# A decode block on one core: one 128-column strip of w3 and one of wo, loaded by sixteen transfers of 15 down to 1 partitions and of 8

## The chip, the cores and the metric

The kernel runs on one core of a Trainium2 chip. The time is device microseconds of one launch. Before the change the median of three runs is 1302.96 us (1302.66 to 1303.77). All arrays are float32.

## The reference, cut to what matters

One token for each of 4 sequences goes through attention over a cache of 4096 positions and 32 heads, and beside it through a small MLP; both are added to the input.

```python
def _A_ref(x, k_cache, v_cache, wq, wo):
    B, Sq, D = x.shape                       # 4, 1, 512
    H, Dh = 32, 128                          # caches: B, H, 4096, Dh
    q = (x @ wq).reshape(B, Sq, H, Dh).transpose(0, 2, 1, 3)
    scores = jnp.einsum("bhqd,bhkd->bhqk", q, k_cache) * (Dh ** -0.5)
    p = _softmax(scores, axis=-1)
    o = jnp.einsum("bhqk,bhkd->bhqd", p, v_cache)
    return o.transpose(0, 2, 1, 3).reshape(B, Sq, H * Dh) @ wo

def _B_ref(x, w1, w2, w3, w4):               # with one token the shifted half adds zeros
    ...
    h2 = _gelu(_layernorm(x1, axis=-1) @ w3) @ w4       # w3: 512 x 1792, w4: 1792 x 512
    return x1 + h2

xn = _layernorm(x, axis=-1)
return x + _A_ref(xn, A_k_cache, A_v_cache, A_wq, A_wo) + _B_ref(xn, B_w1, B_w2, B_w3, B_w4)
```

With one token (S = 1) every shift of the token mixing moves in zeros, so `x1` is the MLP's input and w1 and w2 aren't read.

## The kernel before

**Tiles.** The 128 pairs of sequence and head are worked on four at a time, in 32 steps (`NJ`). A step's keys are one tile of 128 partitions by 64 KB (8.4 MB), loaded as one contiguous row for each partition, and so are its values. There are three such buffers of 64 KB for a partition: `ks[0]` and `ks[1]` for keys in turn, and `vs` for values. Everything else that is large borrows them. At the start w3 (28 KB for a partition) lies in `vs`, with x and the small arrays of the layernorms behind it, wq (64 KB) in `ks[1]`, and the first key tile in `ks[0]`. At the end the last value tile lies in the free key buffer, w4 in `vs`, and wo (64 KB) in `ks[LAST % 2]`, in place of the last keys.

**Engines in a step.** DVE multiplies the key tile by the query, spread over the partitions, in place, and sums over the 128 elements of a head, in two halves (L327 and L328). After each half it raises `summed`. Then it takes the maximum. ACT makes the exponentials (L346). PE multiplies them with the value tile (L380) and sums over partitions (L385, L387); ACT copies the two results out (L351, L353) and raises `done`. Loops on DVE, ACT and PE run by themselves over the 32 steps, tied by semaphores.

**Loads.** All large loads are issued by SP, in the order in which its program has them. At the start stand w3, wq and the first key tile, without a wait. They stand ahead of `tc.close()` and `tc.compile()`, lines 178 and 179, where all engines meet at a barrier; x is loaded by ACT's queue (L180) after that. Then SP has the second key tile (once the q matmuls are through with wq, `pq_ok`), the first value tile (once w3's part and the queries are done), and the third key tile in two halves, each as the half of its buffer has been summed. From there on SP alternates: key tile j + 2 once step j is summed, value tile j + 1 once step j is done. At the end come the last value tile, w4 once step 30 is done, and wo once step 31 is summed.

**Ahead of the steps.** From x two layernorms in a row are made, on DVE with a square root on ACT; `xn` is the attention's input, `x1n` the MLP's. PE transposes each (L213), multiplies `x1n` by w3 (L236), once `w3_in` is there, and then `xn` by wq (L257), once `wq_in` is there. Between them ACT and DVE make the GELU. The queries are scaled (L261), transposed and copied into `qT`; DVE's loop begins with a copy from it (L318).

**The end.** wo is loaded in seven transfers of falling size, each with a semaphore of its own: column blocks 0 to 16, 16 to 24, 24 to 28, 28 to 30, 30 (`wo_cuts`, L286), and the two halves of block 31 (L290). PE waits for each in turn and multiplies (L417, and L151 in `blocks4`, then L432), so that little is left to do when the last one lands. Two stores of half the result each end the program (L439).

**Helpers.** `do` (class `Steps`) records an operation on an engine with its waits. `load(o, i, sem, by, *after, queue="SP")` issues a transfer that adds 16 to `sems[sem]`, and returns the pair to wait for: that semaphore and the value `by`.

Of the kernel before, what the change touches and what calls it, by code (L numbers as in the profile page):

```python
# [44 lines left out]
P = 128  # L45
# [4 lines left out]
PE, DVE, ACT = mybir.EngineType.PE, mybir.EngineType.DVE, mybir.EngineType.Activation  # L50
# [38 lines left out]
def decode_block(ctx: ExitStack, tc: tile.TileContext, x, k, v, wq, wo, w3, w4, out):  # L89
    nc = tc.nc  # L90
    B, H, S, DH = k.shape
    D = wq.shape[0]
    F = w3.shape[1]
    NC = D // P
# [7 lines left out]
    WC = H * DH // P  # L102
    LAST = NJ - 1

    def sb(name, *shape):
        return nc.alloc_sbuf_tensor(name, [P, *shape], F32).ap()
# [4 lines left out]
    ks = [sb(f"ks{n}", R * DH) for n in range(2)]  # L111
    vs = sb("vs", R * DH)
# [35 lines left out]
    def blocks4(start, stop, w, m, src):  # L148

        for t in range(4):  # L150
            i = nc.tensor.matmul(total[32 * t:32 * t + m, :], w, src[:, P * t:P * t + P], start=start, stop=stop)  # L151
        return i

    do = Steps(nc)
    wo_sems = [nc.alloc_semaphore(f"wo{n}") for n in range(7)]
# [4 lines left out]
    wo_cuts = ((0, 16), (16, 24), (24, 28), (28, 30), (30, WC - 1))  # L160
# [3 lines left out]
    def load(o, i, sem, by, *after, queue="SP"):  # L164
        return do(queue, lambda e: e.dma_start(o, i), *after, done=(sems[sem], 16, by))

    do.owned = tc.no_tile_sem_insts
    w3_sb = vs[:, :NC * F].rearrange("p (c f) -> p c f", c=NC)
# [1 line left out]
    xs, lnc = spare[:B, :D], spare[:B, D:2 * D]  # L170
    ident, wide = spare[:, 2 * D:2 * D + P], spare[:, 3 * D:3 * D + NC * 8 * 32]
    wq_sb = ks[1].rearrange("p (c n) -> p c n", c=NC)
    w3_in = load(w3_sb, w3.rearrange("(p c) f -> p c f", c=NC), "w3", 16)
    wq_in = load(wq_sb, wq.rearrange("(p c) n -> p c n", c=NC), "wq", 16)
    k_in = {0: load(ks[0], rows(kf, 0), "k0", 16)}

# [105 lines left out]
    w4_in = load(w4_sb, w4.rearrange("(p m) n -> p m n", m=NF), "w4", 16, DONE[LAST - 1])  # L282
    do.wait("SP", [SUMMED[LAST]])
    wo_r = wo.rearrange("(p c) n -> p c n", c=WC)
    for (c0, c1), sem in zip(wo_cuts, wo_sems):
        nc.sync.dma_start(wo_sb[:, c0:c1], wo_r[:, c0:c1]).then_inc(sem, 16)  # L286
    half = D // 2
    for n, sem in enumerate(wo_sems[-2:]):
# [18 lines left out]
    with nc.Fori(0, NJ // 2, engines=OrderedEngineSet([DVE]), head_slot={DVE: 128}) as j:  # L307
        e, n = nc.vector, 0
# [92 lines left out]
    for m in range(NF):  # L401
        t, g, n = (m, g4[:, m, :], 32) if m < 4 else (m % 4, gT[:, m, :], B)
# [7 lines left out]
    ys = os.rearrange("p m d -> p (m d)")  # L410
    do.wait("PE", [X_ok])
    for (c0, c1), sem in zip(wo_cuts, wo_sems):
        do.wait("PE", [(sem, 16)])
        for c in range(c0, c1):
            if c < 24:
                t = (c + 2) % 4
                i = nc.tensor.matmul(y[32 * t:32 * t + B, :], X[:, c, :], wo_sb[:, c], start=False, stop=(c >= 20))  # L417
            else:
                i = blocks4(False, False, X[:, c, :], B, wo_sb[:, c])
        d = do("PE", lambda e: i)  # L420

        if c1 == 24:
            ys_ok = do("ACT", lambda e: e.copy(ys, y), d)
        elif c1 == 28:
            do.wait("PE", [ys_ok])
            blocks4(False, False, sel, 32, ys)
# [49 lines left out]
```

## Time and profile before

| | us |
|---|---|
| median of three runs | 1302.96 |
| lowest and highest run | 1302.66, 1303.77 |
| the profiled execution, whole | 1302.75 |
| its span, from the first to the last instruction | 1301.4 |

| engine | busy us | share of the span |
|---|---|---|
| DVE | 1164.6 | 89% |
| PE | 365.8 | 28% |
| ACT | 93.5 | 7% |
| POOL | 2.4 | 0% |

The profile is of one execution. PE, PEld (weight loads), DVE, ACT, POOL and SP are the engines; a name with q behind it (SPq) is an engine's sequencer, where DMA issues, waits and branches are. L236 is line 236 of the kernel. A row of the timeline has the start, the duration, the engine and line, what is written and read, the number of instructions merged into the row, and in brackets how long the engine had been idle and what released it. A row of stretches has the length, the busy time and number of instructions of PE, PEld, DVE, ACT and POOL, the granted share of TensorE's clock, the mean busy share of the core's 16 DMA engines, and GB/s. Packets of one DMA engine follow each other; a transfer lands when its semaphore is full.

The DMA moves 561.0 MB from HBM in one launch: 537 MB of keys and values, 8.4 MB each of wq and wo, and 3.7 MB each of w3 and w4.

### The profile page before, as it was taken

The numbers are of one execution on the slowest core, as the hardware profiler recorded it, in microseconds if no ns is written. First come the engines' busy times: TensorE is split into PE (matmuls) and PEld (weight loads), VectorE is DVE, ScalarE is ACT, GpSimd is POOL, SyncE is SP. The second block draws the span as 40 slices with busy tenths as digits, with TensorE's granted clock in tenths as the row PEclk, the third lists the DMA queues.
The fourth block names the chain that finished last, engine by engine and source line by source line (L and its number), as shares of the span: only waits on it lengthen the run. The fifth ranks groups of instructions, "written<-read, shape, count | busy, mean of one in ns | idle before, by whom it ended". The sixth has DMA issues, their size and how long they took to land. (4 is left out here: it accounts for less than half of the span.)

```text
span 1301.4 us, 6682 instructions
## 1 busy us (share of the span) xinstructions
PE 365.8 (28%) x2652; PEld 131.5 (10%) x2652; DVE 1164.6 (89%) x325; ACT 93.5 (7%) x332; POOL 2.4 (0%) x12
## 2 busy tenths in 40 slices
PE   3221233321233321232331133232123322122337
PEld 1000111100011110011110011110001110001112
DVE  3499999999999999999999999999999999999990
ACT  1000000000000000000000000000000000000001
POOL 0000000000000000000000000000000000000000
PEclk9656666655666665666665666665666665566668
DMA  9999999999999999999999999999999999999998
GB/s 403 445 423 447 425 441 425 435 435 431 437 427 443 427 441 425 437 431 435 435 425 443 427 443 425 441 427 433 435 433 437 425 443 427 441 425 437 431 429 369
DMA packets 10831, 561.10 MB, mean 431 GB/s; under 512 B 1212, under 2 KB 1476, under 8 KB 1736
## 3 DMA queue, kind: packets, MB, share of 16 engines
q1 hardware_dynamic: 10808, 561.00, 99.7%
q8 instruction: 4, 0.07, 0.0%
q14 instruction: 3, 0.02, 0.0%
q10 hardware_dynamic: 16, 0.01, 0.0%
HBM read 561.00 MB, written 0.01 MB: 431 GB/s over the span
## 5 line engine op out<-in xcount | busy, mean ns | idle before, releaser
L327 DVE TENSOR_TENSOR ks<-ks,qb 128x8192 f32<-128x8192 f32 x64 | 556.3, 8692 | 59.4 <-DVEq L295 54.4
L328 DVE TENSOR_REDUCE sc<-ks 128x64 f32<-128x8192 f32 x64 | 555.9, 8686 | 2.2
L380 PE MATMUL pv<-vs,pw 128*32 128x512 f32 x1984 | 280.4, 729 | 875.2 <-PEq L295 875.2
L380 PEld LDWEIGHTS pv<-vs,pw 128*32 128x32 f32 x1984 | 77.4, 131 | 1053.6 <-issue 1053.6
L351 ACT COPY os<-pv 128x512 f32<-128x512 f32 x32 | 18.7, 585 | 822.0 <-ACTq L295 822.0
L346 ACT ACTIVATE pw<-sc,small 32x128 f32<-32x128 f32 x128 | 51.0, 398 | 281.2 <-ACTq L295 280.0
L385 PE MATMUL poz<-sel,os 128*128 128x4 f32 x256 | 32.8, 252 | 28.1 <-PEq L295 28.1
L385 PEld LDWEIGHTS poz<-sel,os 128*128 128x128 f32 x256 | 31.0, 191 | 56.3 <-issue 56.3
L346 ACT ACTIVATION_READ_ACCUMULATOR pw<-sc,small 32x1 f32 x128 | 23.5, 184 | 0.0
L434 DVE COPY os<-total 4x128 f32<-4x128 f32 x2 | 0.6, 282 | 15.1 <-PE total L432 15.1
L333 DVE TENSOR_REDUCE small<-sc 128x1 f32<-128x128 f32 x32 | 9.2, 286 | 4.7
L361 DVE RECIPROCAL rz<-oz 128x96 f32<-128x96 f32 (+1 forms) x2 | 1.1, 553 | 13.4 <-ACT oz L353 13.3
L387 PE MATMUL poz<-rs,ones 128*128 128x4 f32 x64 | 11.7, 253 | 0.0
L319 DVE STREAM_TRANSPOSE qb<-qg 128x128 f32<-128x128 f32 x32 | 10.0, 311 | 1.1
L262 DVE STREAM_TRANSPOSE vs<-pw 128x1024 f32<-128x1024 f32 x1 | 1.2, 1246 | 10.4 <-ACT pw L261 10.4
L318 DVE COPY qg<-qT 128x4 f32 x32 | 5.5, 171 | 5.5 <-issue 4.7
L387 PEld LDWEIGHTS poz<-rs,ones 128*128 128x128 f32 x64 | 9.7, 192 | 0.0
L380 PE MATMUL pv<-ks,pw 128*32 128x512 f32 x64 | 9.3, 746 | 0.0
L353 ACT COPY oz<-poz 128x8 f32 x32 | 5.3, 165 | 50.9 <-ACTq L295 50.9
L213 PE MATMUL pt<-vs,pw 4*128 4x4 f32 x16 | 4.0, 372 | 15.8 <-DVE pw L207 15.8
L334 DVE STREAM_TRANSPOSE tr<-small 128x32 f32<-128x32 f32 x32 | 6.8, 212 | 1.1
L417 PE MATMUL y<-ks,X 128*4 128x512 f32 x48 | 7.0, 748 | 2.5 <-DMA ks<-in_A_wo_dram 2.5
(75 smaller groups left out, 72.5 us busy)
## 6 DMA issues: line engine op xcount, KB each, us to landing
ks<-in_A_k_cache_dram SPq DMA_DIRECT2D x2, 4096.0 KB, 26.9
vs<-in_B_w_dram SPq DMA_DIRECT2D x2, 3584.0 KB, 13.8
ks<-in_A_wo_dram SPq DMA_DIRECT2D x1, 4096.0 KB, 21.7
ks<-in_A_wo_dram SPq DMA_DIRECT2D x1, 2048.0 KB, 26.3
ks<-in_A_wo_dram SPq DMA_DIRECT2D x1, 1024.0 KB, 28.3
ks<-in_A_wo_dram SPq DMA_DIRECT2D x1, 512.0 KB, 29.1
ks<-in_A_k_cache_dram SPq DMA_DIRECT2D x31, 42.2
vs<-in_A_v_cache_dram SPq DMA_DIRECT2D x31, 27.0
```

Of the source, the lines that this page charges most:

```text
L318: step(e.tensor_copy(qg, pairs[:, s, bass.ds(j, 1)].rearrange("p o n -> p (o n)")))
L319: step(e.transpose(qb.rearrange("p (n m) -> p n m", m=HP), qg.unsqueeze(2).to_broadcast([P, DH // HP, HP])))
L327: step(e.tensor_tensor(out=kt, in0=kt, in1=qb.unsqueeze(1).to_broadcast([P, w, DH]), op=ALU.mult))
L328: step(e.reduce_sum(sc[s][:, c:c + w], kt, axis=AX.X))
L333: step(e.reduce_max(rm, sc[s], axis=AX.X))
L334: step(e.transpose(tr[s], rm.to_broadcast([P, HP])))
L346: i = nc.scalar.activation(pw[hp, :, 4 * h:4 * h + 4], sc[s][hp, :].rearrange("p (g w) -> p g w", w=4), AF.Exp, bias=small[hp, s, 1:2], sc ...
L351: nc.scalar.copy(os, pv.rearrange("p (m d) -> p m d", m=4)).then_inc(sems["copied"], 1)
L380: i = nc.tensor.matmul(pv[32 * t:32 * t + 32, :], pw[:, g, :], vt[:, 4 * g:4 * g + 4, :], start=(g < 4), stop=(g >= NG - 4))
L385: nc.tensor.matmul(poz[:, 0:G], os[:, m, :], sel.rearrange("p (h m) -> p m h", m=4)[:, m, 0:G], start=(m == 0), stop=(m == 3))
L387: nc.tensor.matmul(poz[:, G:2 * G], ones.to_broadcast([P, P]), rs, start=True, stop=True).then_inc(sems["poz"], 1)
L417: i = nc.tensor.matmul(y[32 * t:32 * t + B, :], X[:, c, :], wo_sb[:, c], start=False, stop=(c >= 20))
```

## The change

`strips` lists sixteen ranges of partitions, of 15, 14, and so on down to 1, and then 8: together 128.

w3 was one transfer of 128 rows of 28,672 bytes. It becomes one of 128 rows of 28,160 bytes, and sixteen transfers for the last 512 bytes of each row (128 columns of float32), one for each range of partitions. All add to the semaphore `w3`, and PE waits for 16 x 17 = 272 instead of 16. All seventeen are issued by SP ahead of wq.

wo's first transfer (column blocks 0 to 16) was 128 rows of 32,768 bytes. It becomes one of 32,256 bytes for each row, and sixteen transfers for the last 512 bytes of each row, with the same ranges. They are issued in its place, ahead of the other six transfers, and PE waits for 272 on that semaphore. Where the bytes come from and where they go in SBUF stays the same.

```diff
--- before.py
+++ after.py
@@ -170,7 +170,14 @@
     xs, lnc = spare[:B, :D], spare[:B, D:2 * D]
     ident, wide = spare[:, 2 * D:2 * D + P], spare[:, 3 * D:3 * D + NC * 8 * 32]
     wq_sb = ks[1].rearrange("p (c n) -> p c n", c=NC)
-    w3_in = load(w3_sb, w3.rearrange("(p c) f -> p c f", c=NC), "w3", 16)
+    sizes, strips = (*range(15, 0, -1), 8), []
+    for n in sizes:
+        p0 = strips[-1][1] if strips else 0
+        strips.append((p0, p0 + n))
+    w3_rows, n3 = w3.rearrange("(p c) f -> p (c f)", c=NC), NC * F - P
+    load(vs[:, :n3], w3_rows[:, :n3], "w3", 16)
+    for n, (p0, p1) in enumerate(strips):
+        w3_in = load(vs[p0:p1, n3:n3 + P], w3_rows[p0:p1, n3:], "w3", 16 * (n + 2))
     wq_in = load(wq_sb, wq.rearrange("(p c) n -> p c n", c=NC), "wq", 16)
     k_in = {0: load(ks[0], rows(kf, 0), "k0", 16)}
 
@@ -282,7 +289,11 @@
     w4_in = load(w4_sb, w4.rearrange("(p m) n -> p m n", m=NF), "w4", 16, DONE[LAST - 1])
     do.wait("SP", [SUMMED[LAST]])
     wo_r = wo.rearrange("(p c) n -> p c n", c=WC)
-    for (c0, c1), sem in zip(wo_cuts, wo_sems):
+    wo_rows, n0 = wo.rearrange("(p c) n -> p (c n)", c=WC), wo_cuts[0][1] * D - P
+    nc.sync.dma_start(ks[LAST % 2][:, :n0], wo_rows[:, :n0]).then_inc(wo_sems[0], 16)
+    for p0, p1 in strips:
+        nc.sync.dma_start(ks[LAST % 2][p0:p1, n0:n0 + P], wo_rows[p0:p1, n0:n0 + P]).then_inc(wo_sems[0], 16)
+    for (c0, c1), sem in zip(wo_cuts[1:], wo_sems[1:]):
         nc.sync.dma_start(wo_sb[:, c0:c1], wo_r[:, c0:c1]).then_inc(sem, 16)
     half = D // 2
     for n, sem in enumerate(wo_sems[-2:]):
@@ -410,7 +421,7 @@
     ys = os.rearrange("p m d -> p (m d)")
     do.wait("PE", [X_ok])
     for (c0, c1), sem in zip(wo_cuts, wo_sems):
-        do.wait("PE", [(sem, 16)])
+        do.wait("PE", [(sem, 16 * (1 + len(strips)) if c0 == 0 else 16)])
         for c in range(c0, c1):
             if c < 24:
                 t = (c + 2) % 4
```

## The prediction

> **What bounds the kernel now.** I read the page first: its DMA lines and the chain of waits.
>
> ```profile
> span 1301.4 us, 6682 instructions
> DMA  9999999999999999999999999999999999999998
> q1 hardware_dynamic: 10808, 561.00, 99.7%
> DVE 3%; DMA 2%; PE 0%; SPq 0%; issue 0%; ACT 0%; DVEq 0%
> ```
>
> Packets of the SP queue fill 99.7% of sixteen DMA engines' time. The chain names DVE because it is followed back only a short way; that isn't the bound. Next, busy time by stretches; the last two numbers of a row are the DMA engines' busy share and GB/s.
>
> ```profile
> 0.00:88.50 88.50, 20.89 (x128) 8.16 (x128) 49.63 (x41) 5.83 (x10) 1.98 (x10) 0.71 0.99 423
> 69.00:1250.00 1181.00, 308.96 (x2220) 110.64 (x2220) 1112.92 (x280) 83.23 (x308) 0.00 (x0) 0.62 1.00 434
> ```
>
> From 69 to 1250 us the engines never pause, at 434 GB/s, 27.1 for each. The time is the bytes through the engines plus two ends. So the change can act in three ways: engine time, a queue that runs empty, or a stage so late that a later load is issued late. Ahead of 88.5 us only 88.5 x (1 - 423/434) = 2.2 us are missing from the steady rate, so hardly anything can be won there. The start by time, SP's queue first and then the engines:
>
> ```profile
> 0.74 0.40 SPq L165 DMA_DIRECT2D vs<-in_B_w_dram  x1
> 1.20 0.42 SPq L165 DMA_DIRECT2D ks<-in_A_wq_dram  x1
> 1.67 0.42 SPq L165 DMA_DIRECT2D ks<-in_A_k_cache_dram  x1
> ```
>
> ```profile
> 2.88 0.20 POOL L183 MEMSET vs<- 128x128 f32 x1 [2.44 <-POOLq L179]
> 2.88 0.56 ACTq L165 DMA_DIRECT2D vs<-in_A_x_dram  x1
> 8.93 0.67 DVE L200 TENSOR_REDUCE lns<-vs 4x1 f32<-4x512 f32 x1 [5.88 <-DMA vs<-in_A_x_dram]
> 21.08 6.03 PE L236 MATMUL y<-vs,lts 128*32 128x448 f32 x32 [0.27 <-DVE lts L216]
> 31.49 1.94 PE L257 MATMUL pv<-ks,X 128*32 128x512 f32 x8 [4.38 <-DMA ks<-in_A_wq_dram]
> 41.45 0.60 ACT L261 ACTIVATE pw<-pv 128x512 f32<-128x512 f32 x1 [11.30 <-PE pq L257]
> 45.70 0.17 DVE L318 COPY qg<-qT 128x4 f32 x1 [0.80 <-DVE qT L264]
> 52.02 8.69 DVE L327 TENSOR_TENSOR ks<-ks,qb 128x8192 f32<-128x8192 f32 x1 [5.79 <-DVEq L295]
> ```
>
> The reader is to see two slacks: PE waits 4.38 us for wq ahead of the q matmuls, and DVE waits 5.79 us for the first K tile. When those loads land is told by the view of the DMA issues (last number: us from issue to landing); its first two lines are the queues' packets, MB and share of the engines in the first 11 us:
>
> ```profile
> q1 hardware_dynamic: 134, 3.87, 88.6%
> q10 hardware_dynamic: 8, 0.01, 0.2%
> vs<-in_B_w_dram SPq DMA_DIRECT2D x1, 3584.0 KB, 11.4
> ```
>
> ```profile
> ks<-in_A_wq_dram SPq DMA_DIRECT2D x1, 30.2
> ks<-in_A_k_cache_dram SPq DMA_DIRECT2D x1, 50.2
> ```
>
> w3 lands at 0.74 + 11.4 = 12.1, wq at 31.4, the first K tile at 51.9. No engine idles between them.
>
> **Part 1: engine time of the strips.** Bytes stay the same; 512 bytes of each of 128 rows become a packet of their own, twice. The trace has no 512-byte packet. The nearest rows are the two halves of wo's last column, 128 rows of 1 KB, so 8 packets for an engine; PE waits for one after the other:
>
> ```profile
> 1298.99 0.10 PEld L432 LDWEIGHTS total<-ks,X 128*4 128x4 f32 x4 [0.23 <-DMA ks<-in_A_wo_dram]
> 1299.32 0.10 PEld L432 LDWEIGHTS total<-ks,X 128*4 128x4 f32 x4 [0.23 <-DMA ks<-in_A_wo_dram]
> ```
>
> They follow each other by 0.33 us, where 128 KB at 434 GB/s take 0.30. So a whole small transfer costs 0.03 us above its bytes. A 512-byte packet takes 0.019 us by its bytes alone and at most that plus 0.03 = 0.049 (all of the extra put down to the transfer's end, which each strip has anew). How are the rows spread? x, four rows, made 8 packets in its queue (q10 above): four of data, four for the semaphore, so four engines. I take it that n rows go to n engines, always from the same one on: the first engine gets a row of all sixteen strips, 16 where it had 8, the last none. First engine: 16 x 0.019 to 0.049 less the 8 x 0.019 = 0.15 it had, +0.15 to +0.63 for a strip. Last: -0.15. For both strips the end moves by -0.3 to +1.3, by which engine finishes last, which no view tells. I take **+0.5**, the middle.
>
> The Trainium skill, "DMA: Bandwidth & Descriptors", section "Why a DMA increments its semaphore by 16 and not by 1", has the same spread: the largest k up to 16 that divides the row count, on the lowest-numbered engines. Its section "Anatomy of one DMA" speaks against the change: each transfer costs some 2.0 us besides its bytes, 32 x 2.0 = 64 us by that, a time near 1367. It is stated for the other descriptor path, and the 0.33 us above disagree for queued transfers.
>
> **Part 2: SP's queue at the start.** Sixteen issues come between w3 and wq. SP's issues there are 0.46 apart. Those of wo:
>
> ```profile
> 1263.29 0.33 SPq L165 DMA_DIRECT2D vs<-in_B_w_dram  x1
> 1267.58 2.50 SPq L286 DMA_DIRECT2D ks<-in_A_wo_dram  x5
> 1270.12 0.90 SPq L290 DMA_DIRECT2D ks<-in_A_wo_dram  x2
> 1289.44 7.03 PE L417 MATMUL y<-ks,X 128*4 128x512 f32 x48 [2.53 <-DMA ks<-in_A_wo_dram]
> 1299.80 0.35 SPq L439 DMA_DIRECT2D out_dram<-os  x1
> 1300.13 0.28 ACTq L439 DMA_DIRECT2D out_dram<-os  x1
> ```
>
> 2.54/5 = 0.51 apart. Transfers of four rows take 0.28 to 0.56 (the stores, and x). So 0.3 to 0.6; I take 0.5, as for back-to-back issues. wq is then issued at 1.20 + 16 x 0.5 = 9.2 instead of 1.20. First packets follow an issue by about 1.0 us:
>
> ```profile
> GB/s 0 0 0 0 0 0 1043 417 104 104 0 0 313 626 521 209 417 626 417 209 521 730 313 209 432 737 313 320 417 730 209 313 521 730 104 417 626 521 209 715
> ```
>
> (eleven microseconds in 40 slices; the seventh begins at 1.65, the issue was at 0.74). So wq's packets can start at 10.2, while w3 keeps the last engine until about 11.8, a little before its landing. The queue doesn't run empty: **0**. The cover is gone at (11.8 - 1.0 - 0.74)/17 = 0.59 us an issue; each 0.1 above costs 1.7 us.
>
> **Part 3: everything behind the barrier.** The three loads stand ahead of a barrier, and POOL's memset at 2.88 waited for it (L179), after SP's last issue ended at 2.09. So the barrier comes 8.0 us later, and x is issued at 10.9. x took 6.05 us (2.88 to 8.93) beside w3's packets of 28.7 KB; now it shares the engines with wq's 64 KB. Lower bound 6.05 again; upper, if all of it scales with the packet, 6.05 x 64/28 = 13.8. x is there at 16.9 to 24.7; middle, 20.8. Then by the old distances: w3 matmuls 12.15 us later, at 33.0; q matmuls at 39.1 instead of 31.49, so 7.6 late; the 4.38 us that PE waited are used up. Who waits for that?
> - The second K load (SP, ahead of which nothing else is queued) needs the q matmuls' end, about 41.4, and then goes out at 49.0, with packets at 50.0. The first K tile keeps the last engine until 51.5. Cost 0; at the upper bound (11.5 late) 54.0 - 51.5 = 2.5 us.
> - The first V load follows at about 52.6, a whole K tile (19 us) ahead of need: 0.
> - DVE's first query copy goes from 45.70 to 53.3, so the scores start at 53.8 instead of 52.02, 1.8 late (5.7 at the upper bound). DVE holds back the fourth K load:
>
> ```profile
> 102.46 0.33 SPq L165 DMA_DIRECT2D vs<-in_A_v_cache_dram  x1
> 123.43 0.33 SPq L165 DMA_DIRECT2D ks<-in_A_k_cache_dram  x1
> ```
>
> ```profile
> vs<-in_A_v_cache_dram SPq DMA_DIRECT2D x1, 26.9
> ```
>
> The V tile ahead of it lands at 129.4; the K packets would start at 124.4 + 1.8 = 126.2. Cover 3 us, so **0**.
>
> **Part 4: wo.** wo's issues go from 7 to 23 and end 8 us later, near 1279. Its column block 16 to 24 is issued at 1276.1, with packets at 1277.1; the engines are at w4 and wo's first block until near 1289 (PE's wait at 1289.44). **0**, with over 9 us of cover. PE waits for all seventeen parts, so it gets the delay of part 1 and no other.
>
> **Sum.** 0.5 + 0 + 0 + 0. The profiled execution took 1302.75 (1301.4 of span and 1.35 around it), so 1303.25. The median of the runs is 0.21 above that execution: **1303.5 us**.
>
> **Rivals**, on the same median.
> - *The odd shapes are slow to issue*, and wq comes late into an empty queue. For it: SP never issued a transfer of few rows in a row of others, and x's took 0.56. Against: the stores' 0.28 and 0.35. At twice 0.42 wq's packets start at 0.74 + 17 x 0.85 + 1.0 = 16.2, 4.4 after w3: 1302.96 + 0.5 + 4.4 = 1307.9, slower. It decides from 0.59 on.
> - *x is stuck behind 64 KB packets* and the second K load comes late: 2.5 + 0.5, 1306.0. For it: x's landing, slow for 8 KB. Against: PE idles less between its two groups of matmuls, and x may meet the strips' short packets.
> - *The rows of a strip crowd on one engine* (the spread isn't what it says): 128 x 0.019 to 0.049, less 0.15, twice: 4.6 to 12.2, some 1311. Against: q10's 8 packets.
> - *Every strip holds the queue as long as a lone transfer*, 1.6 us from the store's issue at 1299.80 to the span's end: 32 x 1.6 = 51, 1354. Against: the 0.33 us.
> - *Engines out of step run faster*: each GB/s above 434 is 561.0/434 - 561.0/435 = 3.0 us, so 1300.0. Against: a row without gaps. The relief of a late last engine alone (-0.3) is no more than no change.
>
> **Numbers.** The forecast 0.66; slow issue 0.14, x 0.09, one engine 0.04, lone transfers 0.02, faster engines 0.05. About 0.2% (2.6 us) is what a measurement of this kernel can tell from no change. So faster 0.05, same 0.66, slower 0.29. The range runs from the forecast's own low end, 1302.96 - 0.3 = 1302.7, less the runs' spread of about half a microsecond, 1302.2, to 1307.0, which takes in x and the milder part of slow issue. The forecast's own range is 1302.2 to 1304.8.
>
> **What would show it.** Strip issues 0.4 to 0.6 apart; wq's issue near 9 and no gap in the packets before it; x's issue near 11 and its landing between 17 and 25; q matmuls near 39; the second K load issued before 50; the scores from 52 to 54; in the tail wo's landings within 1 us of before. A DMA share below 0.97 in a stretch of the first 70 us, or wq landing over 2 us later, would make me wrong; so would a steady rate other than 434.

## The result and the profile after

The changed kernel takes **1305.82 us** (median of 14 runs, 1305.32 to 1306.15) against 1302.99 (14 runs, 1302.55 to 1303.77) beside it: 2.8 us more, a ratio of 1.0021 with a 95% interval of 1.0014 to 1.0029. Forecast were 1303.5 and a range of 1302.2 to 1307.0. The time lies in the range, on the forecast's side of before, and 2.3 us above the forecast. It is also 1.0 us above 1304.8, where the forecast's own range ended.

The page of the changed kernel, its DMA lines and chain of waits (engines, then lines):

```profile
span 1304.4 us, 6714 instructions
DMA  9999999999999999999999999999999999999998
DMA packets 11344, 561.10 MB, mean 430 GB/s; under 512 B 1469, under 2 KB 1989, under 8 KB 2249
q1 hardware_dynamic: 11320, 561.00, 99.6%
DVE 3%; DMA 1%; PE 1%; SPq 0%; issue 0%; DVEq 0%
```

Bytes and busy share are as before. There are 512 packets more: 256 of data and 256 for semaphores. The same two stretches as in the prediction show that the steady part hasn't moved, so the time sits at the two ends:

```profile
0.00:88.50 88.50, 16.75 (x128) 7.60 (x128) 48.40 (x36) 5.35 (x8) 1.98 (x10) 0.77 0.99 421
69.00:1250.00 1181.00, 312.87 (x2220) 111.55 (x2220) 1113.11 (x280) 83.22 (x308) 0.00 (x0) 0.62 1.00 434
```

The start by time, SP's queue and then the engines' steps that the prediction followed:

```profile
0.74 6.32 SPq L165 DMA_DIRECT2D vs<-in_B_w_dram  x17
7.10 0.36 SPq L165 DMA_DIRECT2D ks<-in_A_wq_dram  x1
7.50 35.33 SPq L165 DMA_DIRECT2D ks<-in_A_k_cache_dram  x2
...
8.72 0.56 ACTq L165 DMA_DIRECT2D vs<-in_A_x_dram  x1
...
18.50 0.68 DVE L207 TENSOR_REDUCE lns<-vs 4x1 f32<-4x512 f32 x1 [9.62 <-DMA vs<-in_A_x_dram]
...
30.65 4.83 PE L243 MATMUL y<-vs,lts 128*32 128x448 f32 x32 [0.27 <-DVE lts L223]
...
53.38 8.69 DVE L338 TENSOR_TENSOR ks<-ks,qb 128x8192 f32<-128x8192 f32 x1 [6.12 <-DVEq L306]
```

x comes 9.6 us late and the w3 matmuls with it, yet DVE still waits 6.12 us for the first K tile and starts only 1.36 later than before. That tile and wq themselves land later:

```profile
ks<-in_A_wq_dram SPq DMA_DIRECT2D x1, 25.9
ks<-in_A_k_cache_dram SPq DMA_DIRECT2D x1, 45.7
```

wq lands at 7.10 + 25.9 = 33.0 where it landed at 31.4, the K tile at 53.2 instead of 51.9. SP issued both in time, so the delay is in the engines. The packets of SP's queue that began between 10.8 and 11.9 us, before and after (number, MB, time they took as a share of sixteen engines):

```profile
q1 hardware_dynamic: 32, 1.05, 220.7%
```

```profile
DMA packets 280, 1.11 MB, mean 1011 GB/s; under 512 B 140, under 2 KB 264, under 8 KB 264
q1 hardware_dynamic: 280, 1.11, 301.2%
```

Before, these are wq's first sixteen packets of 64 KB with sixteen semaphore packets: 2.207 x 16 x 1.1 us = 38.8 us, 2.4 for each large one. After, 264 small packets stand beside the sixteen, and all take 53.0 us. In the trace's packet records a small one takes 0.027 us with data and 0.009 for a semaphore, which makes 4.6 for the 124 and 140 of them, and 48.4 remain: **3.03 us for each large packet** in the mean. One by one, eight of the sixteen took 2.42 to 2.62 us and eight took 3.28 to 3.96. From 13.2 to 14.3 us all sixteen engines began their second packet of wq before; after, only eight:

```profile
q1 hardware_dynamic: 16, 1.05, 219.8%
```

```profile
q1 hardware_dynamic: 8, 0.52, 113.6%
```

So half the engines were held, by 0.9 to 1.5 us against the 2.42 of before, though their queues were full. The tail of the changed kernel by time (SP's issues for wo, PE's wait for its first block, PE's last wait):

```profile
1269.13 5.71 SPq L295 DMA_DIRECT2D ks<-in_A_wo_dram  x16
...
1276.69 10.64 SPq L301 DMA_DIRECT2D ks<-in_A_wo_dram  x2
...
1293.24 7.13 PE L428 MATMUL y<-ks,X 128*4 128x512 f32 x48 [5.57 <-DMA ks<-in_A_wo_dram]
...
1302.26 0.10 PEld L443 LDWEIGHTS total<-ks,X 128*4 128x4 f32 x4 [0.18 <-DMA ks<-in_A_wo_dram]
```

PE gets wo's first block at 1293.24 instead of 1289.44, 3.8 us late, of which the start explains 1.6 (wq's delay). Behind that wait PE has only one more, 0.18 us that end at 1302.26; before, the same wait for the last half of block 31 ended at 1299.32 (a row of the prediction). So two things end together, some 2.9 us late: PE's work behind its late first block, and wo's last bytes. e2_tail, below, parts them for wo's strips alone. What the strips' packets did meanwhile is told by the packets that began from 1290.5 to 1292.3 us:

```profile
DMA packets 35, 0.57 MB, mean 319 GB/s; under 512 B 0, under 2 KB 0, under 8 KB 0
```

No small packet is left, of data or for a semaphore; all had begun by 1290.5, and PE still waits until 1293.24, **2.7 us longer**. In the kernel before, where PE started at 1289.44, the last 0.5 us show the same picture (packets that began from 1288.9 to 1289.4), so there the lag is about 0.5 us (0.44 by the records of the last semaphore packet and of the semaphore):

```profile
DMA packets 13, 0.21 MB, mean 426 GB/s; under 512 B 0, under 2 KB 0, under 8 KB 0
```

In the records of the changed kernel the last three semaphore packets of the strips begin 0.03 us apart, and the semaphore's last three increments come 0.17 us apart, from 1292.77 to 1293.11.

### The profile page after: what moved, and what is told of

The parts are those of the page before. It is cut to its first block, busy times and chain, and to the rows that moved or that the text cites. A ratio compares the mean times of both kernels' runs of the same rounds, so it can differ in the third digit from the quotient of the medians.

```text
span 1304.4 us, 6714 instructions
## 1 busy us (share of the span) xinstructions
PE 364.2 (28%) x2652; PEld 131.7 (10%) x2652; DVE 1164.5 (89%) x325; ACT 93.5 (7%) x332; POOL 2.4 (0%) x12
## 5 line engine op out<-in xcount | busy, mean ns | idle before, releaser
L391 PE MATMUL pv<-vs,pw 128*32 128x512 f32 x1984 | 283.9, 736 | 871.4 <-PEq L306 871.4
## 6 DMA issues: line engine op xcount, KB each, us to landing
vs<-in_B_w_dram SPq DMA_DIRECT2D x1, 3584.0 KB, 16.9
```

The costliest lines, as they stand in the source:

```text
L391: i = nc.tensor.matmul(pv[32 * t:32 * t + 32, :], pw[:, g, :], vt[:, 4 * g:4 * g + 4, :], start=(g < 4), stop=(g >= NG - 4))
```

## The experiments

All times are medians beside runs of the kernel before on the same chip, whose medians were 1302.65, 1302.64, 1302.60 and 1302.57 in the four groups.

**One strip at a time: e1_front and e2_tail.** e1_front has the change to w3 alone, e2_tail that to wo alone; the other load is as before.

```diff
# e1_front
...
-    nc.sync.dma_start(ks[LAST % 2][:, :n0], wo_rows[:, :n0]).then_inc(wo_sems[0], 16)
...
+    for (c0, c1), sem in zip(wo_cuts, wo_sems):
...
# e2_tail
-    load(vs[:, :n3], w3_rows[:, :n3], "w3", 16)
...
+    w3_in = load(w3_sb, w3.rearrange("(p c) f -> p c f", c=NC), "w3", 16)
```

> Only w3's strip is split; wo is loaded as before. Theory A (a run of small packets starves the large packet behind it: after the strips wq's first packets lasted about 3.0 us in the mean where they last 2.42 before): slower than before by 0.8 to 1.5 us, and in the stretch from 10.8 to 11.9 us the engines' share is again near 300% instead of 221%. Theory B (x and with it the chain to the second K load come late, behind the barrier): the whole 2.8 us stay, since x is as late. Theory C (the packets' own time alone): +0.3 to +0.6.

> Only wo's strip is split; w3 is loaded as before. Theory A: slower than before by 1.3 to 2.0 us, the first PE wait for wo about 2 us longer than the 2.53 of before, with x, the q matmuls and the first scores where they were. Theory B: as before, within 0.5 us. Theory C: +0.3 to +0.6.

Measured: e1_front 1303.92 (+1.27, ratio 1.0010, 1.0001 to 1.0019), e2_tail 1303.95 (+1.30, same ratio and interval). Each place costs nearly half; together 2.57 of the 2.83. In e1_front the packets from 10.8 to 11.9 us again take 300%:

```profile
q1 hardware_dynamic: 271, 1.11, 299.7%
```

In e2_tail x, the scores and the start are as before, and PE's wait for wo grows:

```profile
51.77 8.69 DVE L336 TENSOR_TENSOR ks<-ks,qb 128x8192 f32<-128x8192 f32 x1 [5.58 <-DVEq L304]
...
1291.53 3.62 PE L426 MATMUL y<-ks,X 128*4 128x512 f32 x32 [2.91 <-DMA ks<-in_A_wo_dram]
...
1300.63 0.10 PEld L441 LDWEIGHTS total<-ks,X 128*4 128x4 f32 x4 [0.22 <-DMA ks<-in_A_wo_dram]
```

PE starts 2.1 us later than before, with nothing changed at the start. Its wait grew by 0.38 us only, and not by the 2 us that were expected, since PE's earlier work ended later too. It catches up: it waits again for later parts, and its last wait ends at 1300.63 instead of 1299.32. These 1.31 us are the whole loss, so here it comes from wo's last bytes, and not from PE's late start. In the packet records 26 of the 128 packets of wo's next part (16 KB each) took over 0.7 us, up to 1.81, where before all took 0.61 to 0.63: the engines are held as they are at the start. Both runs' times fit theory A, the tail's at the lower end. The packets' own time (theory C, at most 0.6) is less than half of either.

**x ahead of the barrier: e8_x_early.** The changed kernel with x's load moved.

```diff
+    x_in = load(xs, x.rearrange("b s d -> (b s) d"), "x", 16, queue="ACT")
     w3_rows, n3 = w3.rearrange("(p c) f -> p (c f)", c=NC), NC * F - P
...
     tc.compile()
-    x_in = load(xs, x.rearrange("b s d -> (b s) d"), "x", 16, queue="ACT")
```

> The changed kernel, but x is issued by ACT ahead of the barrier, so it lands early however long SP issues strips. Theory A: as the changed kernel, 1305.4 to 1306.2, with x landing before 8 us. Theory B: back to 1303.0 to 1303.8. Theory C says nothing of it.

Measured: 1305.47, +2.82 (1.0022, 1.0013 to 1.0031). x's issue, and the first step of the layernorm that uses it:

```profile
0.73 0.57 ACTq L165 DMA_DIRECT2D vs<-in_A_x_dram  x1
...
8.97 0.68 DVE L207 TENSOR_REDUCE lns<-vs 4x1 f32<-4x512 f32 x1
```

The layernorm starts right behind the barrier, as early as before, and all of the loss is still there. Theory B falls.

**Wider rows: e4_wide.** The same staircases, four times as wide.

```diff
+    W = 4 * P
-    w3_rows, n3 = w3.rearrange("(p c) f -> p (c f)", c=NC), NC * F - P
+    w3_rows, n3 = w3.rearrange("(p c) f -> p (c f)", c=NC), NC * F - W
...
```

> The same staircases, but 512 columns wide (2 KB for a row) instead of 128. A packet of 2 KB took 84 ns in the profile of before, so a run of sixteen lasts 1.3 us and not 0.5, time in which the next large packet can be read. Theory A: the packet behind stretches less, by at most 0.7 us; the first engine has 8 more rows of 0.084 for each strip, 0.7 us; together +1.2 to +2.5 over before. Theory C: 2 x (16 x 0.084 - 8 x 0.076) = +1.5 on the first engine, and no stretched packet. If each small transfer had a fixed price instead (theory D), the changed kernel's 2.8 plus what the wider rows add on the first engine, 2 x (16 - 8) x 0.057 = 0.9: +3.7.

Measured: 1306.72, +4.07 (1.0031, 1.0019 to 1.0044). That is more than theory A allowed and a little over theory D. A longer run of packets gave the next large packet no cover. In the packet records all sixteen of wq's first packets took 3.05 to 3.51 us here, so also on the engine that gets no row of the strips. So the number of transfers that an engine gets itself does not explain this run.

**How many transfers in a row: e3_one, e10_4x32, e5_8x16, e6_16x8.** Both strips again, in other cuts.

```diff
# each of the four runs has one of the + lines
-    sizes, strips = (*range(15, 0, -1), 8), []
+    sizes, strips = (128,), []        # e3_one
+    sizes, strips = (32,) * 4, []     # e10_4x32
+    sizes, strips = (16,) * 8, []     # e5_8x16
+    sizes, strips = (8,) * 16, []     # e6_16x8
```

Theories F and G, which one of the expectations names, are put in full with e9_spread below: by F an engine has a lead that covers a few transfers in a row, by G each transfer has its price wherever it stands.

> Both strips as one transfer of 128 rows of 512 bytes instead of sixteen: 8 small packets and one semaphore packet for each engine, where the staircase gives the first engine 16 and 16. So far: e1_front and e2_tail showed +1.3 us each, e8_x_early the whole +2.8 with x early (theory B fell), e4_wide +4.1, more than theory A in its first form allowed. Theory A2 (the read-ahead of an engine holds a limited number of packets, so a long run of small ones leaves little of the next large packet read): a run of 8 is short, no stretched packet, +0.1 to +0.4 over before. Theory D (each small transfer has a fixed price of about 2.8/32 = 0.09): 2 x 0.09, +0.2. Both small here; more than +0.8 speaks against both.

> Both strips by four transfers of 32 rows, two rows and one semaphore packet for each engine. Theory F: four in a row are less than the lead, no stretched packet: +0.2 to +0.5 over before. Theory G: half of e5_8x16's eight, +0.9.

> Each strip by eight transfers of 16 rows: 8 small packets and 8 semaphore packets for every engine, evenly. Theory A2: a run of 16 packets, semaphores counted; the engines with 7 to 9 strips in the changed kernel show hardly any stretch, so +0.2 to +0.9 over before. Theory D: half the transfers, half the price, +1.4.

> Each strip by sixteen transfers of 8 rows: eight engines get 16 small packets and 16 semaphores, eight get none. Theory A2: those eight have the stretched packet in full, +2.4 to +3.4 over before, as the staircase or a little over. Theory D: as the staircase, +2.8. Packets' own time alone (C): +0.6.

Measured, with wq's landing (its issue and the time to landing from the profiles) and PE's start on wo's first block:

| kernel | transfers in a row on an engine | time | over before | wq lands | PE starts on wo |
|---|---|---|---|---|---|
| before | 0 | | | 31.4 | 1289.44 |
| e3_one | 1 | 1302.87 | +0.23 (1.0001, 0.9992 to 1.0010) | 31.5 | 1289.56, ACT last |
| e10_4x32 | 4 | 1303.38 | +0.78 (1.0006, 0.9997 to 1.0015) | 31.5 | 1290.35 |
| e5_8x16 | 8 | 1304.45 | +1.81 (1.0013, 1.0004 to 1.0022) | 31.9 | 1291.69 |
| changed kernel | up to 16 | 1305.82 | +2.83 | 33.0 | 1293.24 |
| e6_16x8 | 16, on half the engines | 1307.34 | +4.70 (1.0035, 1.0022 to 1.0049) | 33.6 | 1295.00 |

The strips' bytes are the same in all five. The first two intervals hold 1, so those two differences are not settled by the times alone. At the start one transfer or four cost wq 0.1 us, eight 0.5 and sixteen 2.2: four pass nearly free, and somewhere between four and eight the price begins. At the tail PE's delay, less that of the start, is 1290.35 - 1289.44 - 0.1 = 0.8 us for four, 2.25 - 0.5 = 1.7 for eight and 5.56 - 2.2 = 3.4 for sixteen: **0.2 us for each transfer in a row**, own packets of some 0.03 among it. So four transfers are covered at the start, where the next work waits for bytes, and not at the tail, where PE waits for the semaphore itself; theory F had expected less for them, and theory G's 0.9 was nearer. PE's late start is not the loss everywhere: in e10_4x32 its last wait for wo ends 0.37 us later than before, while in e5_8x16, e6_16x8 and e8_x_early PE doesn't wait again once it has started, and there the late semaphore sets the end.

The plainest pair is e3_one and e5_8x16. Every engine gets the same eight rows of 512 bytes in each place, by one transfer or by eight, and wq's first packets take 2.42 to 2.58 us in the one and 2.56 to 3.10 in the other (packet records; +0.23 and +1.81 in all). So it is the **transfers** that count, and not the packets.

e6_16x8 holds eight engines and leaves eight: of wq's second packets, eight begin from 13.0 to 14.9 us, where sixteen did in e5_8x16 and before.

```profile
DMA packets 8, 0.52 MB, mean 276 GB/s; under 512 B 0, under 2 KB 0, under 8 KB 0
```

Its strips have eight rows, so rows go one to an engine, on the same engines each time. It is dearer than the staircase, with as many transfers. That in the staircase only the first engine has all sixteen would explain it, but isn't shown: the profile doesn't say which engine a packet belongs to. In the packet records the first packets of wq on the held engines took 3.93 to 4.49 us, the others 2.46 to 2.52.

**Many packets, one transfer: e7_pieces** (w3 alone; 32 small packets on every engine).

```diff
# against the changed kernel; wo's load is as before the change
-    load(vs[:, :n3], w3_rows[:, :n3], "w3", 16)
-    for n, (p0, p1) in enumerate(strips):
-        w3_in = load(vs[p0:p1, n3:n3 + P], w3_rows[p0:p1, n3:], "w3", 16 * (n + 2))
+    w3_r, fm = w3.rearrange("(p c) f -> p c f", c=NC), F - P
+    load(w3_sb[:, :, :fm], w3_r[:, :, :fm], "w3", 16)
+    w3_in = load(w3_sb[:, :, fm:], w3_r[:, :, fm:], "w3", 32)
...
```

> w3 alone, by two transfers: for each row the first 1664 columns of its four chunks, and then the last 128 of all four, 32 small packets of 512 bytes for every engine and one semaphore packet, in a single transfer. Own time: 32 x (0.029 - 0.019) + 24 more packets of 6.7 KB with some 0.01 each = +0.6 on every engine. Theory A2, if any packet counts: the stretch on top, +1.2 to +2.2 over before, and in the stretch of time behind the strips the first packets of wq last 3 us or more. Theory D, or a read-ahead that is used up by transfers or semaphores: +0.4 to +0.7 and wq's packets last 2.42.

Measured: 1303.57, +0.93 (1.0007, 0.9997 to 1.0016). The packets that began from 11.45 to 12.2 us, in which all of wq's first sixteen lie:

```profile
DMA packets 267, 1.17 MB, mean 1559 GB/s; under 512 B 16, under 2 KB 251, under 8 KB 251
## 3 DMA queue, kind: packets, MB, share of 16 engines
q1 hardware_dynamic: 267, 1.17, 393.4%
```

They take 3.934 x 16 x 0.75 = 47.2 us. Sixteen large packets at the 2.42 of before are 38.7; so the 251 small ones have 8.5 at most, 0.034 each. In the packet records the large ones take 2.51 to 2.55, so they are stretched by 0.1 us. wq lands at 2.10 + 30.0 = 32.1, 0.7 late, about the own time that was worked out. The time lies between the two expectations (up to +0.7, and from +1.2), and its interval holds 1; the main load has smaller packets here too. What decides is the large packets: thirty-two small packets in one transfer do not do to them what sixteen in sixteen transfers do. Theory A2 with packets of any kind falls.

**The run broken up: e9_spread** (w3 alone, the strips behind three parts of the main load).

```diff
# against the changed kernel; wo's load is as before the change
-    load(vs[:, :n3], w3_rows[:, :n3], "w3", 16)
-    for n, (p0, p1) in enumerate(strips):
-        w3_in = load(vs[p0:p1, n3:n3 + P], w3_rows[p0:p1, n3:], "w3", 16 * (n + 2))
+    n = 0
+    for (f0, f1), (s0, s1) in zip(((0, n3 // 2), (n3 // 2, n3 * 3 // 4), (n3 * 3 // 4, n3)), ((0, 5), (5, 10), (10, 16))):
+        n += 16
+        load(vs[:, f0:f1], w3_rows[:, f0:f1], "w3", n)
+        for p0, p1 in strips[s0:s1]:
+            n += 16
+            w3_in = load(vs[p0:p1, n3:n3 + P], w3_rows[p0:p1, n3:], "w3", n)
...
```

> w3 alone, with the same sixteen strips, but not in a row: w3's main part is cut in three (1/2, 1/4, 1/4 of its columns), with 5, 5 and 6 strips behind the parts. So far the cost goes with the number of transfers that an engine has in a row, not with packets: one transfer of 128 rows +0.2 (e3_one), 32 small packets in one transfer +0.9 with its own time 0.6 (e7_pieces), eight transfers on every engine +1.8 (e5_8x16), sixteen on eight engines +4.7 (e6_16x8). Theory F (an engine reads ahead of what it writes; each small transfer takes it about 0.2 us on the reading side and 0.03 on the writing side, so a run of more than five or six uses up the lead and the large packet behind waits, and the lead is won back during large packets): runs of five or six cost little, own time 0.3 + 24 more packets with 0.01 each, +0.4 to +0.8 over before. Theory G (a price for each transfer on an engine, wherever it stands): as e1_front, +1.3 or more.

Measured: 1303.40, +0.80 (1.0005, 0.9996 to 1.0014), against e1_front's +1.27 with the same strips in one run. wq lands at 8.09 + 23.9 = 32.0, 1.0 us ahead of e1_front (7.21 + 25.7 = 32.9), though the load is made of two more transfers. It is at the upper end of what theory F gave and under theory G's 1.3. The two kernels' runs don't overlap (1303.20 to 1303.51, and 1303.77 to 1304.16), but they were taken in different groups, and the intervals of the two ratios do overlap.

**Another queue: e11_act_queue** (w3's strips from ACT; wo is loaded as before).

```diff
-        w3_in = load(vs[p0:p1, n3:n3 + P], w3_rows[p0:p1, n3:], "w3", 16 * (n + 2))
+        w3_in = load(vs[p0:p1, n3:n3 + P], w3_rows[p0:p1, n3:], "w3", 16 * (n + 2), queue="ACT")
...
```

> w3's sixteen strips alone, issued from ACT's queue beside SP's main part instead of behind it. The engines then take the small packets in turn with the 28 KB packets of the other queue (as x's packets were in the profile of before), so no run of them forms. Theory F: +0.2 to +0.6 over before. Theory G: +1.3, as e1_front.

Measured: 1331.61, +29.0 (1.0220, 1.0206 to 1.0234): both theories missed it. The timeline and the first stretch:

```profile
7.95 0.26 ACTq L165 DMA_DIRECT2D vs<-in_A_x_dram  x1
...
52.31 0.68 DVE L207 TENSOR_REDUCE lns<-vs 4x1 f32<-4x512 f32 x1 [44.20 <-DMA vs<-in_A_x_dram]
...
77.49 0.33 SPq L165 DMA_DIRECT2D ks<-in_A_k_cache_dram  x1
```

```profile
0.00:88.50 88.50, 17.94 (x128) 7.84 (x128) 19.85 (x32) 5.35 (x8) 1.98 (x10) 0.95 0.67 279
```

x now stands behind the strips in ACT's queue and takes 44 us, so the second K load goes out at 77.5 and the engines idle; 88.5 x (423 - 279)/434 = 29.4 us, the whole loss. In the packet records small packets pass singly between large ones: from 18 to 20 us sixteen packets of 64 KB began and ten small ones, from 20 to 22 sixteen and nine. So an engine that takes packets from two queues in turn lets one small packet through at most for each large one. Ahead of x the first engine has 32 small packets (sixteen strips, each with its semaphore), and SP's queue has 24 large ones for each engine; x's packets begin at 50.7, when the last of these large packets are under way. The run says nothing on F or G. It is the prediction's second rival, at a dose large enough to bite.

**Wider rows, evenly spread: e12_8x16_wide** (e5_8x16 with 2 KB rows).

```diff
-    sizes, strips = (*range(15, 0, -1), 8), []
+    sizes, strips = (16,) * 8, []
+    W = 4 * P
...
```

> e5_8x16 with strips of 512 columns: eight transfers of 16 rows of 2 KB, evenly on all engines. Own time of 8 packets of 0.084 in place of 2 KB more in a large one (0.076), and 8 semaphore packets: +0.1 for each strip. Theory F in terms of time (about 0.2 us on the reading side for each transfer; the writing side now takes 0.09 of it): the lead lasts longer, little stretch, +0.2 to +0.8 over before. If it is dearer than e5_8x16's +1.8 or equal, wider rows hide nothing, as e4_wide already had it (+4.1 against +2.8), and the price of a transfer is not a fixed time that other work of the engine can cover.

Measured: 1304.91, +2.34 (1.0018, 1.0009 to 1.0027), dearer than e5_8x16's 1.81 by half a microsecond. wq lands at 5.06 + 27.0 = 32.1 (31.9 there). Four times the data in each transfer covers nothing of its price. Theory F as a matter of reading ahead in time falls too; what is left of it is the count: four to six transfers in a row cost the next large packet little, and further ones about 0.2 us each. e4_wide does not fit this count.

## Why the prediction was right, and where its size was off

The range and the side held, the likeliest case did not: 0.66 stood on no change, and the ratio of 1.0021 lies at the 0.2% bound, its interval wholly above 1. That the time still lies in the range is luck: the forecast's own range ended at 1304.8, and the rest, up to 1307.0, was there for a late x and for slow issue, and neither cost anything. Of the signs that were named, the steady rate, the DMA share and wq's landing (1.6 us late, under 2) stayed within their bounds; "wo's landings within 1 us of before" did not, since they came 2.9 to 3.8 us late.

**Part 1, the engine time of the strips, was mis-sized**: +0.5 us forecast (at most 1.3), 2.8 measured. The own time of the packets was right (0.027 us, and 0.009 for the semaphore's, where 0.019 to 0.049 was taken). The wrong step was to read the price of a small transfer from wo's two halves, 0.33 us apart for 8 packets each, and to add it up: those transfers last longer than the 0.2 us that one costs in a run, so their price can lie hidden under their bytes. That explanation fits, but no run tries it alone. What the runs show is the price: at 0.2 us for each transfer, sixteen on an engine are 3.2 us, where their packets take 16 x 0.036 = 0.58. An estimate from the four to six transfers that pass nearly free is that the engine goes on for about a microsecond ahead of them; then the large packet behind is held, by up to 1.5 us in the changed kernel. The prediction put the halves' extra down to "the transfer's end", which may be the right place, but its bound of 0.03 us was taken where a transfer's bytes last longer than 0.2 us, and does not hold for strips whose packets are shorter.

**Part 2 was right.** Issues are 0.37 us apart ((7.10 - 0.74)/17), not 0.5; wq is issued at 7.10 and its packets wait for nothing but the engines. The rival of slow issue falls.

**Part 3 was right.** x came 9.78 us after its issue, between the bounds 6.05 and 13.8, at 18.5 (16.9 to 24.7); the scores started at 53.38 (52 to 54); e8_x_early shows that none of the loss hangs on it. Two steps on the way were off: x was issued at 8.72 and not at 10.9, and the q matmuls began at 35.31 and not at 39.1, since PE's two groups of matmuls ran back to back and faster. The second K load still came in time.

**Part 4 was wrong in its last sentence.** "PE waits for all seventeen parts, so it gets the delay of part 1 and no other": PE's first wait for wo grew from 2.53 to 5.57 us, since it waits for the semaphore, which fills 2.7 us after the last small packet has begun. Whether this costs time depends on whether PE can catch up: in e2_tail it does, and the loss is the late bytes. The cover for SP's issues held: SP was blocked for 10.6 us in the last two issues (L301), with over 8 us still to go before those bytes were due.

**The other rivals.** Rows of a strip crowding on one engine: no, with strips of eight rows e6_16x8 has eight engines held and eight free. A price for each transfer on the queue: yes, but 0.2 us for each further transfer in a row on an engine, and not the 1.6 of a lone one. The Trainium skill's 2.0 us a transfer ("DMA: Bandwidth & Descriptors", section "Anatomy of one DMA"), which it states for the other descriptor path, is ten times what these runs show in a queue. Its reason, that the semaphore is updated only when the last byte is confirmed to have landed, fits the late semaphore at the tail, though the trace doesn't show when the bytes land. Faster engines out of step: no, 434 GB/s as before.

**What stays open.** Why a transfer in a run takes 0.2 us, and whether it is the semaphore's increment or another part of a transfer's end: a transfer without one was not tried. Why wider rows make it dearer, and why e4_wide costs 1.2 more than the changed kernel, of which the first engine's own time is 0.9, and holds wq's first packet on every engine. The two strips alone add up to 2.57, and together cost 2.8; the rest is within the intervals, and so is no finding. No cut of the strips beat the kernel before: one transfer of 128 rows comes nearest (+0.23, not told from no change).

## What to carry to other kernels

In a queue that keeps the DMA engines full, count the transfers that one engine gets in a row, not only bytes and packets: here four to six small ones passed nearly free ahead of the next large load, and further ones cost about 0.2 us each, and rows four times as wide did not lessen it. A consumer that waits for the last of them waits for the semaphores, 0.2 us for each in the run. If a load must be cut by columns, cut it into few transfers of many rows: one strip of 128 rows in each place cost +0.23 us, not told from no change (e3_one). Don't put many small transfers in a second queue beside large packets when something waits behind them: x came 44 us after its issue in e11_act_queue.

## What the runs showed of the hardware that was not expected

- A semaphore can fill long after the last packet has begun: 2.7 us behind a run of up to sixteen small transfers, 0.44 behind a large one. The last increments of such runs come 0.17 to 0.20 us apart (the changed kernel, e5_8x16, e6_16x8).
- The price of a run is not linear at its start: wq landed 0.1 us late behind four transfers on each engine, 0.5 behind eight, 2.2 behind sixteen.
- Two queues on the same engines take turns by packets, 64 KB against 512 bytes: 8 KB behind sixteen strips in a second queue took 44 us.
- A run of small transfers holds the large packet behind it on the same engine: eight of wq's first packets took 3.28 to 3.96 us instead of 2.42.
- SP can be held in an issue: its last but one for wo took 9.7 us, with 22 transfers ahead of it since w4, where the same line's issues took 0.42 before. The count alone isn't the measure: in e10_4x32 the last issue took 4.4 us with eleven ahead, and at the start of e9_spread twenty went out at 0.35 to 0.44 each. The changed kernel's issues of the two halves (ns min, median and max, and the first and last start):

```profile
L301 SPq DMA_DIRECT2D ks<-in_A_wo_dram x2: 899/5298/9698, 1276.7 to 1286.4; - x2
```
